# A two-level Strassen product at the end of a fused attention and feed-forward kernel: five store buffers, earlier differences, a PSUM bank read out in another way

## The chip, the cores and the metric

The kernel runs on one core of a Trainium2 chip. The metric is the device time of one execution in microseconds, and the time given for a kernel is the median of several executions. A profiled execution also has a span, from its first instruction to its last; its own time is a little longer than that.

The engines are named as the profile names them: PE (TensorE, matmuls), PEld (its weight loads), DVE (VectorE), ACT (ScalarE), POOL (GpSimd) and SP (SyncE, here only an issuer of DMAs). [...]

## The reference

```
q, k, v: (8, 12, 448, 64) float32; w_in: (768, 2048); w_out: (2048, 768)
q_n, k_n = rmsnorm(q, g_q), rmsnorm(k, g_k)
attn = softmax(q_n @ k_n^T / sqrt(64)) @ v          # per batch and head
x = attn.transpose(0, 2, 1, 3).reshape(3584, 768)
h = x @ w_in
out = relu(h)^2 @ w_out                             # (3584, 768) float32
```

What matters here is the last line: g = relu(h)^2 times w_out.

## The kernel before, in words

The eight batches are taken two at a time, in four spans of 896 tokens. For each span the kernel computes attention, then the first product (x times w_in, with the activation, giving g), then the second product (g times w_out). Both products use the Winograd form of Strassen's algorithm with seven products of half-size blocks instead of eight: g is cut into g11, g12, g21 and g22 by feature halves and batches. It lies transposed in `gT` (16 rows of features, each with 448 tokens of the one batch and 448 of the other), and the differences of g that the form needs lie in `gC` (three sets of eight rows).

In spans 0 to 2 the second product of a span is spread under the attention of the next. In span 3 no attention is left, and `last_product` computes the second product alone. It applies the Winograd form a second time, inside each of the seven products, to two of the three output column blocks of 128; the third column block is computed plainly. The change is in this function.

`last_product` runs its seven products in the order A11, A12, S2, S1, S3, A22, S4 (`order`, index `o`). For each of them PE runs, in this order:

- **pa** (a11 times b11: 8 matmuls of 224 columns), which ACT copies to p1i (L1264);
- **the third block** `ps`, 16 matmuls of 448 columns (`third`, L1235), which DVE or ACT adds or copies into its place (L1239 and L1241);
- **pb**, **pc** and **pd**, 8 matmuls each, with the sums of weights s1 to s4 and the differences of g t1 to t4;
- then **pa** again (a12 times b21 on top of the first value), **pd** again (a22 times t4 on top) and **pc** again (s4 times b22 on top).

DVE makes zi = p1i + pb (L1275) and yi = zi + pc (L1279). `based` (L1254) lets POOL add the base, a block of an earlier product's result, to these: za and zb from zi, yb from yi. `meet` (L1247) is the DVE addition that takes one quarter out of PSUM: yb + pd after pd's first use, base + pa, za + pd after its second use, zb + pc. PE may only run pd a second time when the addition yb + pd has read the bank, since the second use adds to the value in it. In the product S3 (`both`) the quarters go to two extra buffers, `blocks`, and POOL adds these to two bases (`settle`, L1259).

Around this core, for the next product: `add_g` (L1191) makes one of the four differences of g on DVE (896 elements wide, into `ts`), `add_weights` (L1179) makes the four sums of weights on POOL, and `load_set` (L1170) fetches a set of weights of w_out by a DMA on SP. `combine` makes the differences in `gC` from one row of g: four DVE instructions of 448 elements, two in part 0 (L1028 and L1029) and two in part 1 (L1031 and L1032).

`deliver` sends one finished block to HBM: DVE transposes it in squares of 32 into a store buffer `osb` (L1139), and four DMAs of 56 KB each take it out (L1142). The pool has two such buffers. The blocks m = 1 and 0 of a product that leaves are delivered "late", in the next product behind the third block's sum; the third block itself is sent at once. In the last product (`end`) the blocks go as soon as they are there, with the DMAs on SP and ACT in turn, and block 0 in two halves.

The order of instructions on each engine is the order in which the code issues them. Waits between engines and for buffers come from the tile framework.

Of the kernel before, what the change touches and what calls it, by code (L numbers as in the profile page):

```python
# [10 lines left out]
F32 = mybir.dt.float32  # L11
# [376 lines left out]
def attention_then_ffn_bounded(  # L388
# [35 lines left out]
    nc = tc.nc  # L424

    B, H, S, D = q.shape
    NT, DM = out.shape
    DFF = w_in.shape[1]
    P = 128
# [3 lines left out]
    NFC = DFF // P  # L433
    HALF = DM // 2
    HC = NPAIR // 2
    HF = NFC // 2
    NSPAN = B // 2
# [27 lines left out]
    qk, qkT, ident, mhalf, gains, rstd0, _ = held  # L465
    gT = consts.tile([P, NFC, 2 * S], F32, name="gT")
    xT = consts.tile([P, 2, NPAIR, S], F32, name="xT")
    xC = consts.tile([P, 3, HC, S], F32, name="xC")
    gC = consts.tile([P, 3, HF, S], F32, name="gC")
# [24 lines left out]
    A11, S2, S1, S3, A12, A22, S4 = range(7)  # L494
# [526 lines left out]
    def combine(f, parts=(0, 1)):  # L1021


        g11, g12 = gT[:, f, 0:S], gT[:, f, S:2 * S]
        g21, g22 = gT[:, HF + f, 0:S], gT[:, HF + f, S:2 * S]
        sub = nc.vector.tensor_tensor
        if 0 in parts:
            sub(gC[:, 0, f], g12, g11, ALU.subtract)  # L1028
            sub(gC[:, 1, f], g22, gC[:, 0, f], ALU.subtract)  # L1029
        if 1 in parts:  # L1030
            sub(gC[:, 2, f], g21, gC[:, 1, f], ALU.subtract)  # L1031
            sub(g12, g22, g12, ALU.subtract)  # L1032
# [101 lines left out]

    rows = out.rearrange("(b g t) n -> b t g n", b=B, t=32)

    def deliver(work, span, ct, col, t, queues=(nc.sync,), part=slice(0, S // 32)):
        osb = work.tile([P, S // 32, 32], F32, tag="osb", name="osb")[:, part]
        nc.vector.transpose(osb.rearrange("p g n -> p (g n)"), ct[:, part.start * 32:part.stop * 32])  # L1139
        for i in range(0, P, 32):  # L1140
            queue = queues[i // 32 % len(queues)]
            queue.dma_start(rows[2 * span + t, :, part, col * P + i:col * P + i + 32], osb[i:i + 32])  # L1142

    def last_product(pool):
# [4 lines left out]
        HK, HS = HF // 2, S // 2  # L1149
# [5 lines left out]
        left = [[qf[:, NW2:NW2 + NS], qf[:, NW2 + NS:NW2 + 2 * NS], tf[:, 0:NS], tf[:, NS:2 * NS]],  # L1155
                [xf[:, 4 * NT2 + n * NS:4 * NT2 + (n + 1) * NS] for n in range(3)] + [tf[:, 2 * NS:3 * NS]]]
        ts = [[t[:, n * NT2:(n + 1) * NT2].rearrange("p (c n) -> p c n", c=HK) for n in range(4)] for t in (cf, xf)]
        dead = [gT[:, f, 0:S] for f in range(NFC)]
        used, late = [0], []
        sub, add = ALU.subtract, ALU.add  # L1160

        def weights_of(o, m, k):
# [18 lines left out]
        def parts_of(o):  # L1181
            rhs = rhs_of[order[o]]
            return [[rhs[:, k * HK:(k + 1) * HK, t * HS:(t + 1) * HS] for t in range(2)] for k in range(2)]

        def add_g(o, n):
            if o == len(order):
                return
            (b11, b12), (b21, b22) = parts_of(o)
            t1, t2, t3, t4 = ts[o % 2]
            dst, x, y = ((t1, b12, b11), (t2, b22, t1), (t3, b22, b12), (t4, b21, t2))[n]  # L1190
            nc.vector.tensor_tensor(dst, x, y, sub)  # L1191
# [4 lines left out]
        work = yield load_set, add_weights, add_g  # L1196

        p1s = [work.tile([P, S], F32, tag="p1", name="p1", bufs=HC) for _ in range(HC)]
        ys = dead[0:HC]
        blocks = [work.tile([P, S], F32, tag="block", name="block") for _ in range(2)]  # L1200

        def place():
            used[0] += 1
            return dead[HC - 1 + used[0]]

        def run(ps, lhs, rhs, first=True):
            for c in range(HK):
# [4 lines left out]
        for o, i in enumerate(order):  # L1212
            end = o + 1 == len(order)
            (b11, b12), (b21, b22) = parts_of(o)
            (a11, a12), (a21, a22) = [[weights_of(o, m, k) for k in range(2)] for m in range(2)]
            s1, s2, s3, s4 = sums_of(o)
            t1, t2, t3, t4 = ts[o % 2]

            into = {A11: [(None, p1s)], A12: [(p1s, None)], S2: [(p1s, p1s)], S1: [(p1s, ys)],
                    S3: [(ys, None), (p1s, p1s)], A22: [(p1s, None)], S4: [(ys, None)]}[i]  # L1220
            leaves = any(dst is None for _, dst in into)
            into = [(base, dst or [place() for _ in range(HC)]) for base, dst in into]
            at = ((HC if i in (S3, A22) else 0), 1 if i in (S3, S4) else 0)

            def send(m, part=slice(0, S // 32)):
                deliver(work, NSPAN - 1, into[0][1][m], m + at[0], at[1],
                        (nc.sync, nc.scalar) if end else (nc.sync,), part)

            both = len(into) > 1

            def third():
                m = HC - 1
                ps = bank("ps")
                for c in range(HF):
                    nc.tensor.matmul(ps, weights_of(o, m, c // HK)[:, c % HK], rhs_of[i][:, c],  # L1235
                                     start=c == 0, stop=c == HF - 1)
                for base, dst in into:
                    if base is None:
                        nc.scalar.copy(dst[m], ps)  # L1239
                    else:  # L1240
                        nc.vector.tensor_tensor(dst[m], base[m], ps, add)  # L1241

            def meet(m, t, left, ps):

                part = slice(t * HS, (t + 1) * HS)
                dst = blocks[m] if both else into[0][1][m]
                nc.vector.tensor_tensor(dst[:, part], left, ps, add)  # L1247

            def based(m, t, x, name):
                base = into[0][0]  # L1250
                if both or base is None:
                    return x
                y = small_of(name)
                nc.gpsimd.tensor_tensor(y, x, base[m][:, t * HS:(t + 1) * HS], add)  # L1254
                return y

            def settle(m):
                for base, dst in into if both else ():
                    nc.gpsimd.tensor_tensor(dst[m], base[m], blocks[m], add)  # L1259

            pa = ps_s.tile([P, 2, 512], F32, tag="s", name="pa")[:, 0, 0:HS]
            run(pa, a11, b11)
            p1 = small_of("p1i")
            nc.scalar.copy(p1, pa)  # L1264
            third()
            add_g(o + 1, 0)
            for args in late:
                deliver(*args)
            late[:] = []
            if leaves:  # L1270
                send(HC - 1)
            pb = ps_o.tile([P, S], F32, tag="o", name="pb")[:, 0:HS]
            run(pb, s2, t2)
            z, y = small_of("zi"), small_of("yi")
            nc.vector.tensor_tensor(z, p1, pb, add)  # L1275
            z21, z12 = based(1, 0, z, "za"), based(0, 1, z, "zb")
            pc = bank("pc")[:, 0:HS]
            run(pc, s1, t1)
            nc.vector.tensor_tensor(y, z, pc, add)  # L1279
            y22 = based(1, 1, y, "yb")  # L1280
            add_g(o + 1, 1)
            pd = ps_o.tile([P, S], F32, tag="t", name="pd")[:, 0:HS]
            run(pd, s3, t3)
            add_weights(o + 1)
            meet(1, 1, y22, pd)
            run(pa, a12, b21, False)
            if both or into[0][0] is None:
                nc.scalar.copy((blocks if both else into[0][1])[0][:, 0:HS], pa)
            else:
                meet(0, 0, into[0][0][0][:, 0:HS], pa)  # L1290
            add_g(o + 1, 2)
            run(pd, a22, t4, False)
            meet(1, 0, z21, pd)
            settle(1)
            if end:
                send(1)
                send(0, slice(0, HS // 32))
            run(pc, s4, b22, False)
            meet(0, 1, z12, pc)
            settle(0)  # L1300
            if end:
                send(0, slice(HS // 32, S // 32))
            elif leaves:
                for m in (1, 0):
                    late.append((work, NSPAN - 1, into[0][1][m], m + at[0], at[1]))
            add_g(o + 1, 3)
            load_set(o + 2)
        yield

# [66 lines left out]
    with tc.tile_pool(name="last_product", bufs=2, reuse_waits="tile") as last:  # L1376
        rest = last_product(last)
        load_set, add_weights, add_g = next(rest)
        with tc.tile_pool(name="first_product", bufs=2, reuse_waits="tile") as work:
            for u, _ in enumerate(first_product(work, NSPAN - 1)):  # L1380
                if u in (14, 21):
                    load_set(u // 7 - 2)
                if u == N1 // 2:
                    add_weights(0)
                if u == N1 - 2:
                    add_g(0, 0)
                    add_g(0, 1)
                if u == N1 - 1:
                    add_g(0, 2)
                    add_g(0, 3)  # L1390
                    combine(HF - 1)
        with tc.tile_pool(name="second_product", bufs=2, reuse_waits="tile") as work:
            rest.send(work)

# [87 lines left out]
```

## Time and profile before

| | us |
|---|---|
| median of 3 runs | 1368.57 (1367.56 to 1369.83) |
| the profiled execution's own time | 1369.07 |
| its span | 1367.1 |
| PE busy | 1335.5 (98%) |
| DVE, ACT, POOL busy | 875.6, 431.8, 627.2 |
| mean granted PE clock | 0.992 |
| first matmul of the last product | 1227.68 |
| last matmul's modelled end | 1357.81 |

The profile gives every instruction with its start, its duration and, in brackets, how long its engine stood idle before it and what ended that. The ends of matmuls are modelled. A table of stretches gives each engine's busy time between two moments, with the clock that was granted to PE (1.00 is full speed).

### The profile page before, as it was taken

Reading aid. Unit: us, or ns where it says so; the run is one execution under the profiler, and the core shown is the slowest. Engines: PE = TensorE matmul, PEld = TensorE weight load, DVE = VectorE, ACT = ScalarE, POOL = GpSimd, SP = SyncE. Lnnn points to the kernel's source line nnn. Section 1 sums busy time; section 2 is a strip of 40 time slices with the busy share of each in tenths; the row PEclk is TensorE's granted clock in tenths of the full one; section 3 lists DMA queues with packets and bytes.
Section 4 is the critical chain, followed back from the end, with each engine's and each line's share of the span. In section 5 each row is a group of like instructions: output and inputs, shape, how many; then the busy total and the mean of one; then the engine's idle time right before and its main releaser. Section 6 shows DMA issues by size and latency. Waiting matters only on the chain.

```text
span 1367.1 us, 17241 instructions
## 1 busy us (share of the span) xinstructions
PE 1335.5 (98%) x5770; PEld 671.9 (49%) x5770; DVE 875.6 (64%) x1535; ACT 431.8 (32%) x681; POOL 627.2 (46%) x505
## 2 busy tenths in 40 slices
PE   8999999999999999999999999999999999999986
PEld 3333445444444554544444455444444455557865
DVE  6999788599987334477788423467787623336442
ACT  7886466433332111233333011233333111110000
POOL 5667533466573123555564122645666312424541
PEclk9999999999999999999999999999999999999997
DMA  9777999655675333355676433344765435312332
GB/s 239 214 220 197 319 362 322 181 128 109 132 149 128 97 88 90 100 114 123 141 143 119 111 93 90 100 109 108 153 125 115 102 99 182 87 58 67 111 101 37
DMA packets 413815, 190.15 MB, mean 139 GB/s; under 512 B 282389, under 2 KB 408725, under 8 KB 413717
## 3 DMA queue, kind: packets, MB, share of 16 engines
q1 hardware_dynamic: 406164, 180.21, 51.0%
q0 software_dynamic: 4736, 8.40, 2.5%
q8 instruction: 48, 0.79, 0.2%
q10 hardware_dynamic: 2816, 0.34, 0.2%
q14 instruction: 51, 0.41, 0.1%
HBM read 155.72 MB, written 33.16 MB: 138 GB/s over the span
## 4 chain that ended last, share of the span: by engine, by line
PE 87%; DVE 7%; ACT 2%; issue 1%; DMA 1%; POOL 1%; SPq 0%; DVEq 0%; ACTq 0%; POOLq 0%
PE ps L1106 28%; PE pd L1068 10%; PE pa L1068 10%; PE pc L1068 10%; PE sc L785 7%; PE pav L862 7%; PE pb L1068 5%; PE ps L1235 3%; PE pd L1208 1%; ACT gT L797 1%; PE pc L1208 1%; PE pa L1208 1%; DVE gT L810 1%; PE sc L793 1%; DVE rstd L715 1%
## 5 line engine op out<-in xcount | busy, mean ns | idle before, releaser
L1106 PE MATMUL ps<-gT,sw 128*128 128x448 f32 x576 | 225.8, 543 | 0.0
L1044 POOL TENSOR_TENSOR gT<-gT 128x448 f32<-128x448 f32 x96 | 93.7, 978 | 284.6 <-ACT gT L1040 284.6
L750 POOL TENSOR_TENSOR half<-half,mhalf 128x28 f32<-128x28 f32 x36 | 176.1, 4891 | 71.7 <-DVE half L749 68.5
L1106 PE MATMUL ps<-gC,sw 128*128 128x448 f32 x432 | 170.1, 543 | 0.0
L1106 PEld LDWEIGHTS ps<-gT,sw 128*128 128x128 f32 x576 | 107.5, 190 | 113.9 <-issue 110.2
L1068 PE MATMUL pa<-xT,sw 128*128 128x448 f32 x384 | 155.0, 540 | 0.6 <-ACT p L1072 0.6
L1040 ACT ACTIVATE gT<-gT 128x448 f32<-128x448 f32 x96 | 55.3, 577 | 313.9 <-DVE gT L1083 313.9
L1106 PEld LDWEIGHTS ps<-gC,sw 128*128 128x128 f32 x432 | 80.6, 190 | 86.3 <-issue 83.7
L787 ACT ACTIVATE pr<-sc 128x896 f32<-128x896 f32 x87 | 77.5, 915 | 121.8 <-PE sc L785 121.8
L785 PE MATMUL sc<-qkT 64*64 64x448 f32 (+1 forms) x1152 | 109.7, 496 | 0.0
L1068 PEld LDWEIGHTS pa<-xT,sw 128*128 128x128 f32 x384 | 72.8, 190 | 72.7 <-issue 70.5
L583 POOL TENSOR_TENSOR gC<-gC 128x384 f32<-128x384 f32 x64 | 76.4, 1212 | 62.1 <-DVE gC L579 60.4
L1083 DVE TENSOR_TENSOR gT<-z,pd 128x448 f32<-128x448 f32 x32 | 19.8, 620 | 97.8 <-PE pd L1068 97.7
L830 POOL DMA_DIRECT2D xT<-factors x72 | 38.1, 534 | 92.3 <-DMA factors<-square 55.3
L1068 PE MATMUL pd<-xT,sw 128*128 128x448 f32 x192 | 77.9, 542 | 1.4 <-DVE z L1075 1.4
L1068 PE MATMUL pd<-xC,sw 128*128 128x448 f32 x192 | 77.5, 540 | 1.3 <-DVE gT L1083 1.3
L1068 PE MATMUL pb<-xC,sw 128*128 128x448 f32 x192 | 77.5, 540 | 0.2 <-DVE gT L1083 0.2
L1068 PE MATMUL pc<-xC,sw 128*128 128x448 f32 x192 | 77.4, 539 | 0.0
L1068 PE MATMUL pc<-xT,sw 128*128 128x448 f32 x192 | 77.4, 539 | 0.0
L752 POOL TENSOR_TENSOR qk<-qk,half 128x448 f32<-128x448 f32 x72 | 75.5, 1068 | 2.8
L862 PE MATMUL rest<-pr,vt 64*64 64x448 f32 x348 | 72.7, 537 | 0.0
L862 PE MATMUL pav<-pr,vt 64*64 64x448 f32 x348 | 72.7, 537 | 0.0
(223 smaller groups left out, 2176.8 us busy)
## 6 DMA issues: line engine op xcount, KB each, us to landing
sw<-w1s SPq DMA_DIRECT2D x224, 192.0 KB, 2.4
sw<-w2s SPq DMA_DIRECT2D x126, 256.0 KB, 3.3
w1s<-gC SPq DMA_DIRECT2D x8, 1344.0 KB, 7.2
w2s<-gC SPq DMA_DIRECT2D x8, 1344.0 KB, 6.2
out_dram<-osb SPq DMA_DIRECT2D x184, 56.0 KB, 1.8
qk<-in_q_dram SPq DMA_DIRECT2D x144, 56.0 KB, 3.6
qk<-in_k_dram SPq DMA_DIRECT2D x144, 56.0 KB, 2.9
xT<-factors POOLq DMA_DIRECT2D x72, 112.0 KB, 3.4
```

Source lines behind the costliest of these rows:

```text
L583: nc.gpsimd.tensor_tensor(*[blocks_of(n)[:, place_of(n, i)] for i in (dst, x, y)], op)
L750: nc.gpsimd.tensor_tensor(half, half, mhalf, ALU.pow)
L752: nc.gpsimd.tensor_tensor(qkn[:, s], raw[:, s], half[:, s * NG:(s + 1) * NG].rearrange("p g -> p g ()").to_broadcast([P, NG, 32]), ALU.mult)
L785: nc.tensor.matmul(sc[part, h, 0:n], qkT[rows, 0, 1, keys], qkT[rows, 0, 0, of], start=True, stop=True)
L787: nc.scalar.activation(pr, sc[:, :, 0:n], AF.Exp)
L862: nc.tensor.matmul(into, vs[i][rows, h, c, :], probs[i, c][rows, h, :], start=(c == 0), stop=(c == NF), skip_group_check=True)
L1040: nc.scalar.activation(g, src, AF.Relu)
L1044: nc.gpsimd.tensor_tensor(g, g, g, ALU.mult)
L1068: nc.tensor.matmul(ps, stream[n + at][:, c], rhs[:, c], start=first and c == 0, stop=c == HC - 1, skip_group_check=not first)
L1106: nc.tensor.matmul(ps, stream[n][:, c % 4], rhs_of[i][:, c], start=c == 0, stop=c == HF - 1)
L1208: nc.tensor.matmul(ps, lhs[:, c], rhs[:, c], start=first and c == 0, stop=c == HK - 1, skip_group_check=not first)
L1235: nc.tensor.matmul(ps, weights_of(o, m, c // HK)[:, c % HK], rhs_of[i][:, c], start=c == 0, stop=c == HF - 1)
```

## The change

The change does five things in `last_product` and `deliver`:

1. The store buffer `osb` of the last product gets five buffers instead of two (`kept`).
2. Three differences of g for the next product are issued ahead of the third block, and so are the late deliveries; the fourth comes behind yi.
3. Where a product has a base and one destination, pd is read out by adding the base to it; y is added to the result afterwards, in place, on POOL (on DVE in the last product). yb is gone.
4. The results of A12, S3, A22 and S4 and the two `blocks` get fixed rows of `gT` and `gC` that are no longer read; the separate `block` buffers are gone.
5. The second part of `combine` for the last row of g moves from ahead of the last product to the end of its first stage.

```diff
-    def deliver(work, span, ct, col, t, queues=(nc.sync,), part=slice(0, S // 32)):
-        osb = work.tile([P, S // 32, 32], F32, tag="osb", name="osb")[:, part]
+    def deliver(work, span, ct, col, t, queues=(nc.sync,), part=slice(0, S // 32), kept=2):
+        osb = work.tile([P, S // 32, 32], F32, tag="osb", name="osb", bufs=kept)[:, part]
...
-        dead = [gT[:, f, 0:S] for f in range(NFC)]
-        used, late = [0], []
+        dead = [gT[:, f, 0:S] for f in range(HF)] + [gC[:, 1, f] for f in range(HF)]
+        late = []
...
-        blocks = [work.tile([P, S], F32, tag="block", name="block") for _ in range(2)]
-
-        def place():
-            used[0] += 1
-            return dead[HC - 1 + used[0]]
+        blocks = dead[2 * HF - 2:]
+        homes = {A12: dead[HC:2 * HC], S3: dead[HF:HF + HC], A22: dead[HF + HC:HF + 2 * HC], S4: dead[HC:2 * HC]}
...
-            into = [(base, dst or [place() for _ in range(HC)]) for base, dst in into]
+            into = [(base, dst or homes[i]) for base, dst in into]
...
             run(pa, a11, b11)
             p1 = small_of("p1i")
             nc.scalar.copy(p1, pa)
-            third()
-            add_g(o + 1, 0)
+            for n in range(3):
+                add_g(o + 1, n)
             for args in late:
                 deliver(*args)
             late[:] = []
+            third()
             if leaves:
                 send(HC - 1)
...
             nc.vector.tensor_tensor(y, z, pc, add)
-            y22 = based(1, 1, y, "yb")
-            add_g(o + 1, 1)
+            add_g(o + 1, 3)
             pd = ps_o.tile([P, S], F32, tag="t", name="pd")[:, 0:HS]
             run(pd, s3, t3)
             add_weights(o + 1)
-            meet(1, 1, y22, pd)
+            if both or into[0][0] is None:
+                meet(1, 1, y, pd)
+            else:
+                meet(1, 1, into[0][0][1][:, HS:S], pd)
+                x = into[0][1][1][:, HS:S]
+                (nc.vector if end else nc.gpsimd).tensor_tensor(x, x, y, add)
             run(pa, a12, b21, False)
...
-            add_g(o + 1, 2)
             run(pd, a22, t4, False)
...
-                    late.append((work, NSPAN - 1, into[0][1][m], m + at[0], at[1]))
-            add_g(o + 1, 3)
+                    late.append((work, NSPAN - 1, into[0][1][m], m + at[0], at[1], (nc.sync,), slice(0, S // 32), 5))
+            if o == 0:
+                combine(HF - 1, (1,))
             load_set(o + 2)
...
-                    combine(HF - 1)
+                    combine(HF - 1, (0,))
```

`send` passes the five buffers to `deliver` in the same way.

More of the change, by code (lines that the diff above doesn't have):

```diff
@@ L1226, in send @@
                 deliver(work, NSPAN - 1, into[0][1][m], m + at[0], at[1],
-                        (nc.sync, nc.scalar) if end else (nc.sync,), part)
+                        (nc.sync, nc.scalar) if end else (nc.sync,), part, 5)
             both = len(into) > 1
```

## The prediction

> **What bounds the kernel now.** I looked first at the page: TensorE (PE) is busy for 1335.5 of 1367.1 us, so whatever PE does not wait for is free. The change touches only the last product and what leads into it, so I cut that end of the trace at the starts of its seven pa blocks (numbered stage 0 to 6 below) and asked for busy times by stretch. Columns: stretch, length, then busy time of PE, weight loads, VectorE (DVE), ScalarE (ACT), GpSimd (POOL), granted clock, DMA share and GB/s.
>
> ```profile
> span 1367.1 us, 17241 instructions
> ...
> 1227.68:1246.26 18.58, 16.88 (x74) 13.55 (x73) 16.50 (x16) 1.69 (x4) 8.38 (x6) 1.00 0.03 4
> 1246.26:1262.93 16.67, 16.67 (x73) 13.55 (x72) 7.88 (x12) 0.35 (x1) 6.27 (x6) 1.00 0.37 110
> 1262.93:1280.06 17.13, 16.87 (x73) 13.55 (x73) 8.80 (x13) 0.35 (x1) 9.27 (x8) 1.00 0.43 118
> 1280.06:1296.67 16.61, 16.61 (x73) 13.64 (x73) 8.17 (x11) 0.35 (x1) 9.64 (x8) 1.00 0.29 97
> 1296.67:1313.28 16.61, 16.61 (x74) 13.64 (x74) 7.67 (x12) 0.69 (x2) 9.49 (x7) 1.00 0.36 109
> 1313.28:1336.81 23.53, 19.14 (x74) 15.39 (x73) 9.92 (x14) 0.35 (x1) 12.80 (x11) 0.85 0.35 94
> 1336.81:1357.81 21.00, 18.72 (x73) 14.72 (x71) 6.41 (x13) 0.35 (x1) 1.89 (x3) 0.92 0.23 36
> 1357.81:1367.10 9.29, 0.00 (x0) 0.00 (x0) 0.80 (x2) 0.00 (x0) 0.00 (x0) 0.61 0.36 55
> ```
>
> Stages 3 and 4 never wait: 16.61 us, which is seven blocks of 1.51 and the third block's 6.01. The others show what can be won: 1.97 in stage 0, 0.06 in stage 1, 0.52 in stage 2, 6.92 in stage 5, 4.22 in stage 6 (against 16.78, since its last block is counted to its modelled end), and the 9.29 after PE's last matmul. The timeline of PE says where each loss sits: always at the second use of the pd bank.
>
> ```profile
> 1243.12 1.78 PE L1208 MATMUL pd<-xC,qk 128*128 128x224 f32 x8 [1.70 <-DVE p L1247]
> 1276.93 1.78 PE L1208 MATMUL pd<-xC,qk 128*128 128x224 f32 x8 [0.26 <-DVE p L1247]
> 1331.41 3.36 PE L1208 MATMUL pd<-xT,wb 128*128 128x224 f32 x8 [4.39 <-DVE gT L1247]
> 1352.83 3.12 PE L1208 MATMUL pd<-xC,qk 128*128 128x224 f32 x8 [2.28 <-DVE gT L1247]
> ```
>
> All wait for L1247, the addition that reads pd's first value (`meet(1, 1)`); PE may not add to the bank before it. VectorE's own timeline says what held that addition back in the last two stages, and what held the last store back:
>
> ```profile
> 1327.14 0.65 DVE L1139 STREAM_TRANSPOSE osb<-gT 128x448 f32<-128x448 f32 x1 [3.43 <-DMA out_dram<-osb]
> ...
> 1330.97 0.39 DVE L1247 TENSOR_TENSOR gT<-yb,pd 128x224 f32<-128x224 f32 x1 [1.16 <-POOL yb L1254]
> ...
> 1352.38 0.39 DVE L1247 TENSOR_TENSOR gT<-yb,pd 128x224 f32<-128x224 f32 x1 [1.51 <-POOL yb L1254]
> ...
> 1361.16 0.41 DVE L1139 STREAM_TRANSPOSE osb<-gT 128x224 f32<-128x224 f32 x1 [2.93 <-DMA out_dram<-osb]
> ```
>
> The third delivery of a stage waits until one of two store buffers has left (3.43 us); zi, yi, then GpSimd's za, zb, yb queue up behind it. That is one chain: buffer, zi, yb, pd.
>
> **What the Trainium skill says.** "SBUF — State Buffer", "Who interferes with whom": a VectorE instruction with two SBUF inputs contends with a GpSimd instruction that reads SBUF; the loser blocks for the whole of the other's instruction. The trace agrees, and this sets my price for stage 0:
>
> ```profile
> 1236.80 1.57 DVE L1031 TENSOR_TENSOR gC<-gT,gC 128x448 f32<-128x448 f32 x1
> 1238.29 1.68 DVE L1032 TENSOR_TENSOR gT<-gT 128x448 f32<-128x448 f32 x1
> ...
> 1236.24 1.65 POOL L1179 TENSOR_TENSOR xT<-wb 128x512 f32<-128x512 f32 x1
> 1237.85 1.65 POOL L1179 TENSOR_TENSOR qkT<-wb,xT 128x512 f32<-128x512 f32 x1
> ```
>
> The same two instructions take 0.62 us at 1226.2. Beside GpSimd, each ends 0.48 after the GpSimd instruction does, and GpSimd's next ends some 1.15 later: they alternate. "TensorE: Matmul & The Clock Gate", "What's actually happening": a free-running window of about 3.4 us; one that is idle halves PE's clock until a busy one has passed. Here too, with a threshold:
>
> ```profile
> 1325.80:1329.20 3.40, 1.22 (x7) 0.87 (x5) 1.96 (x4) 0.00 (x0) 1.00 (x2) 1.00 0.65 100
> 1329.20:1332.60 3.40, 1.19 (x3) 1.12 (x4) 2.24 (x4) 0.00 (x0) 3.32 (x4) 0.50 0.34 55
> 1240.40:1243.80 3.40, 1.70 (x10) 1.35 (x9) 3.30 (x6) 0.35 (x1) 0.00 (x0) 1.00 0.00 0
> ```
>
> A window with 1.22 us of work (2.2 idle) was followed by half clock; one with 1.70 (1.7 idle) was not.
>
> **The change, part by part.**
>
> *Five store buffers.* Stages 5 and 6 deliver three and six blocks; the wait was for a transfer of two deliveries ago (landing 1.9 us after issue, four issues of 0.49 on SP). With five, only the sixth delivery of stage 6 reuses one, of some 15 us before. The waits of 3.43, 3.23 and 2.93 go. Late next in stages 5 and 6: nothing, see pd.
>
> *pd freed without GpSimd.* VectorE adds the base to pd at once (0.39, one SBUF input, so no lock). GpSimd's yb (0.66) becomes an in-place addition of y (0.66), queued behind `add_weights` (four of 1.3 to 2.0); in stage 6 VectorE does it, 0.39, beside PE's pa. With B as the end of pb: zi ends at B+0.4, yi at B+1.9, the base goes on at the end of pd, B+3.0, done by B+3.4; PE wants pd at B+4.5. So stages 2, 5 and 6 lose nothing: **−0.52, −6.92, −4.22**, half clock of stages 5 and 6 included. Who waits for the late addition: only the next stage's transposes of that block, after stages 1 and 5. GpSimd ends it near B+8.7; VectorE comes to the transposes at B+8 (stage 6) to B+11; the third sum behind them is due at B+15.1. Covered by the third block's 6.01; without it, up to 0.7.
>
> *Differences ahead.* Three 896-wide instructions (1.08 each alone, up to twice that beside GpSimd) and two transposes (0.6) fill 4.5 to 6.5 of the 7.5 us until the third sum is ready, where VectorE stood idle for 5.4 to 6.2. Free there. The eight DMAs of a late delivery keep their place on SP: behind the last `load_set`, ahead of the third block's four; they pass nothing. The fourth difference (index 3) takes the place of the second between yi and `meet(1, 1)`. There `add_weights` starts as zb ends (B+1.75), so the difference waits for one GpSimd instruction (to B+3.0), ends at B+4.0, and the base addition ends at B+4.4 against 4.5. On a knife's edge: 0 to 0.3 in each of stages 1, 2, 3, 5; I take **+0.3** in all.
>
> *Stage 0 gets worse.* Behind the combine's first half (ends 1236.76) stood two 448-wide subtractions and one difference before zi; now three differences. In the alternating pattern: first behind GpSimd's third weight sum (1237.89 + 0.97), GpSimd's fourth (1240.04), second (1241.0), third (1242.0); it was 1240.98. So zi, yi, the fourth difference and pd come 1.0 later: **+1.0** (bounds 0 and +1.5). PE's idle time becomes 2.7, and half clock may follow. In this execution's window 1240.4 to 1243.8 only 1.0 of work would be left, under the 1.22 above. Over free phases, with a threshold of 2.0 idle, (3.41 + 2.7 − 4.0) / 3.41 = 62%. It halves some 3 us of work: **+1.5** when it comes. The combine's second half (two of 0.62) at the end of stage 0 takes the place of a 1.08 difference; stage 1 has 7 us free: 0.
>
> *Results in rows of g, blocks too.* The rows now used (gC's second third after S2; gT's first rows after A11) were last read a stage or more earlier, so no wait: 0 (bounds 0 and +0.5). No instruction is added.
>
> *The tail.* It is 9.29: 0.4 for the sum, 2.93 waiting for a buffer, 0.41 transpose, 0.9 for two issues on each of SP and ACT, 2.5 landing, 2.6 to the end. The wait goes, but the last four DMAs then stand behind the eight just before: on each queue 0.3, 1.46 (this trace's odd long one; 0.49 normally), 0.5, 0.5 from E−0.4, E being the modelled end of the last matmul; so they issue at E+1.4 to 2.4 and the end comes at E+6.8 to 7.8. "DMA: Bandwidth & Descriptors", "Issuing engines are not separate DMA queues", says that SP and ACT share the 16 engines; that costs little here: the eight DMAs before the last four made up some 2.5 us of full DMA share (0.13, 0.72, 0.51, 0.99 and 0.10, microsecond by microsecond from 1357). Taken: 7.3, **−2.0** (−1.5 to −2.5).
>
> Sum: 1.0 + 1.5 + 0.3 − 0.52 − 6.92 − 4.22 − 2.0 = −10.9. The profiled execution took 1369.07 (span and 1.97 around it), so 1358.2; it stands 0.5 above the median of the three runs, 1368.57. In their terms **1357.7 us**.
>
> **Rivals.**
> - *No half clock in stage 0*: 1.5 less, 1356.2. The window's phase decides; 1.0 of work against 1.22 speaks for the half clock.
> - *Stage 0 hardly grows*, if VectorE gets two turns to GpSimd's one: 1355. Against it: the strict alternation above.
> - *The knife's edge cuts*: a second GpSimd instruction (1.3) slips in before the fourth difference in stages 1, 2, 3 and 5, each costing about 1: 1361.5. The alternation speaks against it.
> - *It doesn't do what it says*: the third delivery still waits some 3.4 us in stage 5, for SP's queue of issues instead of a buffer: 1361. SP has 5.8 us of issues there (12 of 0.49), but VectorE needn't wait for issues, only for free buffers.
> - *Slower*: GpSimd's late addition stands behind `add_weights`, and that behind the next set's transfer. If it comes after B+15, VectorE stops at the late transposes with the third sum, zi and pd behind it, in stages 2 and 6. From 6.4 us of delay on it costs one for one; to turn the 12 us won into a loss it must be 13 late in each. The only such wait shown is 2.45 (a set landing 6.5 after issue). At 13 late: about 1371.
>
> **How the numbers follow.** The forecast has 0.48, no half clock 0.27, stage 0 unchanged 0.08, knife's edge 0.10, stores still waiting 0.04, slower 0.03. Likeliest case alone: 1356.7 to 1359. Adding the others until under 2 in 10 is left out: 1354.5 to 1361. What a measurement can tell from no change is about 0.2%, 2.7 us; every case but the last is beyond it, with a little left for two bad ones together: faster 0.95, same 0.02, slower 0.03.
>
> **What would show it.** Right: no transpose waiting for out_dram; stages 2 to 6 at 16.6 to 16.8; stage 0 at 19.5, or 21 at half clock; GpSimd gone from pd's waits; under 8 us after the last matmul. Wrong: a wait at pd over 0.5 in a stage other than 0, a stage 0 under 18.6, or VectorE waiting for GpSimd at a late transpose.

## The result, and the profile after

The changed kernel takes 1360.93 us (median of 5, 1359.77 to 1361.38) against 1368.57 (median of 5): a ratio of 0.994, with a 95% interval of 0.9926 to 0.9955. It is faster by 0.6%, clear of noise, and inside the range of the prediction (1354.5 to 1361), but by less than 0.1 us: it lies 3.2 us above the forecast of 1357.7.

The profiled execution took 1361.38, with a span of 1359.1. Cut at the starts of the seven pa blocks as before (same columns: stretch, length, busy time of PE, weight loads, DVE, ACT, POOL, granted clock, DMA share, GB/s):

```profile
1228.54:1249.49 20.95, 18.27 (x74) 14.69 (x72) 16.49 (x15) 1.69 (x4) 8.89 (x6) 0.92 0.03 4
1249.49:1266.20 16.71, 16.71 (x74) 13.56 (x74) 9.75 (x14) 0.34 (x1) 6.86 (x6) 1.00 0.36 110
1266.20:1282.93 16.73, 16.73 (x73) 13.55 (x72) 9.14 (x13) 0.34 (x1) 7.58 (x8) 1.00 0.44 122
1282.93:1299.64 16.71, 16.71 (x74) 13.56 (x74) 8.01 (x11) 0.34 (x1) 7.60 (x8) 1.00 0.27 95
1299.64:1316.24 16.60, 16.60 (x73) 13.63 (x72) 7.64 (x12) 0.69 (x2) 6.60 (x7) 1.00 0.35 109
1316.24:1332.85 16.61, 16.61 (x73) 13.64 (x73) 11.26 (x14) 0.35 (x1) 11.94 (x10) 1.00 0.51 132
1332.85:1349.62 16.77, 16.77 (x73) 13.45 (x72) 6.10 (x13) 0.35 (x1) 2.35 (x4) 1.00 0.28 44
1349.62:1359.10 9.48, 0.00 (x0) 0.00 (x0) 0.80 (x2) 0.00 (x0) 0.00 (x0) 0.71 0.35 55
```

Stages 5 and 6, which took 23.53 and 21.0, are at the floor (16.61, and 16.78 for stage 6). Stage 0 has grown from 18.58 to 20.95. The tail, forecast at 7.3, is 9.48: it has not shrunk at all. PE waits for pd in stage 0 alone.

Stage 0 in the timeline. The first three lines are the three differences that now stand ahead of zi, then the two sums of weights on GpSimd that run beside them, then PE's second use of pd:

```profile
1237.57 2.18 DVE L1191 TENSOR_TENSOR xT<-gT 128x896 f32<-128x896 f32 x1
...
1239.78 2.04 DVE L1191 TENSOR_TENSOR xT<-gT,xT 128x896 f32<-128x896 f32 x1
...
1241.75 1.08 DVE L1191 TENSOR_TENSOR xT<-gT 128x896 f32<-128x896 f32 x1
...
1237.12 1.68 POOL L1179 TENSOR_TENSOR xT<-wb 128x512 f32<-128x512 f32 x1
...
1238.76 2.12 POOL L1179 TENSOR_TENSOR qkT<-wb,xT 128x512 f32<-128x512 f32 x1
...
1244.97 3.17 PE L1205 MATMUL pd<-xC,qk 128*128 128x224 f32 x8 [2.68 <-DVE p L1244]
```

Two differences take 2.18 and 2.04 us beside GpSimd, and the third takes 1.08 once GpSimd is done: the engines take turns. PE stands for 2.68 us and then runs its eight matmuls in 3.17 instead of 1.78, for the most part at half clock.

The tail in the view of who waited for whom on SP's queue, from 1340 us on (total, times, longest):

```profile
SPq L1142 <- DVE osb L1139: 10.2, 3, 6.8
SPq L1142 <- DMA out_dram<-osb: 1.5, 2, 1.1
```

No transpose waits for a transfer any more; instead the issue of one DMA waits for the landing of another. The trace names for each DMA its semaphore, the counter that its landing raises: the twelve of the tail share eight. SP's issue at 1352.93 takes over the semaphore of a DMA that ACT issued at 1349.32, and starts 0.02 us after that one has landed, at 1352.91. It is not the number under way that holds it. SP begins to wait at 1351.78, when six are under way and two of the eight semaphores are free; those two go to ACT's next issues, at 1351.84 and 1352.40. The one buffer wait became two semaphore waits, 1.5 us together.

### The profile page after: what moved, and what is told of

Its sections match the earlier page's. It is cut to its first block, busy times and chain, and to the rows that moved or that the text cites. A ratio compares the mean times of both kernels' runs of the same rounds, so it can differ in the third digit from the quotient of the medians.

```text
span 1359.1 us, 17239 instructions
## 1 busy us (share of the span) xinstructions
PE 1334.0 (98%) x5770; PEld 671.3 (49%) x5770; DVE 875.7 (64%) x1536; ACT 431.7 (32%) x681; POOL 621.4 (46%) x504
## 4 chain that ended last, share of the span: by engine, by line
PE 89%; DVE 6%; ACT 3%; issue 1%; DMA 0%; POOL 0%; DVEq 0%; ACTq 0%
PE ps L1106 28%; PE pd L1068 10%; PE pa L1068 10%; PE pc L1068 10%; PE sc L785 7%; PE pav L862 7%; PE pb L1068 5%; PE ps L1232 3%; PE pd L1205 2%; PE pc L1205 1%; PE pa L1205 1%; ACT gT L797 1%; DVE gT L810 1%; PE sc L793 1%; DVE rstd L715 1%
```

## The experiments

Each kernel was timed in five rounds beside the kernel before, and ratios are to that. Stages are those of its profiled execution.

**Is it the order in stage 0?** (e1) The changed kernel with:

```diff
-            for n in range(3):
+            for n in range(3) if o else ():
                 add_g(o + 1, n)
...
-            add_g(o + 1, 3)
+            if o:
+                add_g(o + 1, 3)
...
             if o == 0:
+                for n in range(4):
+                    add_g(1, n)
+            if o == 1:
                 combine(HF - 1, (1,))
```

> The changed kernel, but in stage 0 no difference of g stands ahead of the third block: all four for the next product come at the end of stage 0, and the combine's second half for the last row comes at the end of stage 1 instead of stage 0. Theory (stage 0 pays for differences that VectorE makes in turn with GpSimd's sums of weights, and then for half clock): stage 0 falls from 20.95 us to 16.6 to 17.0, no half clock follows, stage 1 stays within 0.3 of 16.71; in all 4.0 to 4.4 us less than the changed kernel, some 1356.7. Rival (pd's first value is late in stage 0 for another reason, such as the g rows that the last squares on GpSimd leave late): stage 0 stays above 19, in all less than 2 us gained.

Measured: 1355.57 us, ratio 0.9901 (0.9885 to 0.9916). Stage 0 by stretch, and VectorE in it:

```profile
1226.87:1243.48 16.61, 16.61 (x74) 13.63 (x73) 10.50 (x11) 1.69 (x4) 8.04 (x6) 1.00 0.03 5
```

```profile
1234.37 1.58 DVE L1029 TENSOR_TENSOR gC<-gT,gC 128x448 f32<-128x448 f32 x1
1236.18 0.39 DVE L1273 TENSOR_TENSOR zi<-p1i,pb 128x224 f32<-128x224 f32 x1 [0.22 <-PE pb L1205]
1237.62 0.39 DVE L1277 TENSOR_TENSOR yi<-zi,pc 128x224 f32<-128x224 f32 x1 [1.06 <-PE pc L1205]
```

VectorE now waits for PE, not the other way round, and stage 0 is at its floor: 4.34 us less than in the changed kernel, and 1.97 less than before. Both the old loss and the new one were differences and combines in VectorE's way. The four differences fit behind it: stage 1 takes 16.70. The median fell by 5.4 us, 1.0 more than I expected at most; the stages and the tail account for 4.4 of it, and the last product began 1.7 us earlier in this profile, which is within the scatter of its start (see the end of the next section).

**What holds the tail: DMAs under way, or bytes?** (e2) The changed kernel with block 0 of the last product sent whole, after the last matmul: the same bytes, later, in eight DMAs instead of twelve.

```diff
             if end:
                 send(1)
-                send(0, slice(0, HS // 32))
...
             if end:
-                send(0, slice(HS // 32, S // 32))
+                send(0)
```

> The changed kernel, but block 0 of the last product leaves whole after the last matmul, in four DMAs, instead of in two halves with four DMAs each: eight DMAs in the tail instead of twelve, with the same bytes, and the first half leaving later. Theory A (the tail stayed at 9.5 us because the ninth and later DMAs wait until an earlier one, whose semaphore they take over, has landed: eight can be under way): no DMA waits for another, the tail falls from 9.48 to 7.2 to 8.0 us, in all 1.5 to 2.3 less. Theory B (bytes: the 16 DMA engines with pieces of 128 bytes are the bound): the tail is the same or longer, 9.5 to 10.5, since the bytes start later.

Measured: 1358.84 us, 0.9922 (0.9908 to 0.9935). The tail by stretch:

```profile
1350.05:1357.77 7.72, 0.00 (x1) 0.00 (x0) 1.03 (x2) 0.00 (x0) 0.00 (x0) 0.77 0.45 68
```

9.48 has become 7.72, though the first half of block 0 starts later. The bytes are not the bound. SP waits for no landing in it, as theory A said, but four issues are gone too, and e2 does not part the two. The record of the queues gives an estimate: the last issue ends 5.12 us after the last matmul in the changed kernel and 3.09 here, and SP's two waits are 1.5 of these 2.03.

(e3) The other way: each half as soon as it is there, in sixteen DMAs.

```diff
                 (nc.vector if end else nc.gpsimd).tensor_tensor(x, x, y, add)
+            if end:
+                send(1, slice(HS // 32, S // 32))
...
                 meet(0, 0, into[0][0][0][:, 0:HS], pa)
+            if end:
+                send(0, slice(0, HS // 32))
...
-                send(1)
-                send(0, slice(0, HS // 32))
+                send(1, slice(0, HS // 32))
```

> The changed kernel, but in the last product each half of blocks 1 and 0 leaves as soon as it is there (four deliveries of four small DMAs each, in the order 1 right, 0 left, 1 left, 0 right). Theory A (eight DMAs under way at most): the first two groups have landed when the third and fourth want their semaphores, so the tail falls from 9.48 to 6.0 to 7.0 us, in all 2.5 to 3.5 less. Theory B (bytes): the bytes start about 2 us earlier, so the tail falls too, to 7 to 8.5. A third possibility (the issue cost of 0.5 us for each DMA decides): 16 instead of 12 issues, the tail stays at 9 or more.

Measured: 1361.05 us, 0.9932 (0.9918 to 0.9945); the tail is 9.97. My own numbers for theory A missed: I had the first groups landed in time. They were not, since both queues draw on the same semaphores, and SP's first DMA of the tail, at 1349.62, had to wait for one that ACT had issued 3.0 us before. SP's queue from 1340 us on:

```profile
SPq L1142 <- DMA out_dram<-osb: 10.5, 3, 4.9
```

Of the three possibilities the third gave the right tail, but not for its reason alone. Of the 10.5 us of waiting for landings only 0.8 falls behind the last matmul; the other waits held SP back before it. So SP's eight issues, which take 4.4 us together, nearly all came behind the last matmul, and the last of them ended 5.5 us after it. With 8, 12 and 16 DMAs the tails are 7.7, 9.5 and 10.0; but the number does not decide alone: the runs with twelve go from 9.29 (before) to 11.35 (e5). In every run the end comes 4.1 to 5.0 us after the last issue has ended.

**Which part brought the gain?** (e4) The changed kernel with two buffers and with yb on GpSimd again. What is left is the order, and the places of results.

```diff
-                        (nc.sync, nc.scalar) if end else (nc.sync,), part, 5)
+                        (nc.sync, nc.scalar) if end else (nc.sync,), part, 2)
...
             nc.vector.tensor_tensor(y, z, pc, add)
+            y22 = based(1, 1, y, "yb")
             add_g(o + 1, 3)
...
-            if both or into[0][0] is None:
-                meet(1, 1, y, pd)
-            else:
-                meet(1, 1, into[0][0][1][:, HS:S], pd)
-                x = into[0][1][1][:, HS:S]
-                (nc.vector if end else nc.gpsimd).tensor_tensor(x, x, y, add)
+            meet(1, 1, y22, pd)
...
-                    late.append((work, NSPAN - 1, into[0][1][m], m + at[0], at[1], (nc.sync,), slice(0, S // 32), 5))
+                    late.append((work, NSPAN - 1, into[0][1][m], m + at[0], at[1], (nc.sync,), slice(0, S // 32), 2))
```

> The changed kernel with two of its parts undone: two store buffers again, and yb again on GpSimd ahead of pd; only the new order (three differences and the late deliveries ahead of the third block) and the new places of results are left. Theory A (the order alone lets the late deliveries leave early, so the buffer wait comes while PE works, and zi is early enough that GpSimd's yb is covered): stages 1 to 4 and 6 at 16.6 to 17.0, stage 5 at most 1.5 us longer, tail within 0.7 of 9.48; in all 0 to 2.5 us slower than the changed kernel. Theory B (the prediction's parts: the buffers bring the 3.43 and 3.23 of waiting, pd without GpSimd the rest): stages 5 and 6 go back to some 20 us or more, in all 6 to 11 us slower.

Measured: 1361.02 us, 0.9946 (0.9932 to 0.996), not to be told from the changed kernel's 0.994. Stages 3, 5 and 6:

```profile
1280.21:1296.82 16.61, 16.61 (x74) 13.64 (x73) 7.53 (x11) 0.35 (x1) 7.71 (x8) 1.00 0.27 97
...
1313.43:1331.16 17.73, 16.87 (x74) 13.55 (x73) 11.30 (x14) 0.34 (x1) 11.51 (x10) 1.00 0.47 123
1331.16:1347.91 16.75, 16.75 (x73) 13.43 (x71) 5.61 (x12) 0.34 (x1) 3.33 (x5) 1.00 0.28 44
```

The order alone does nearly all: 5.80 of the 6.92 in stage 5, everything in stage 6. My parts list had given these to the buffers and to pd. (The new places of results and the moved half of `combine` are in this run too; no run has the order without them.)

(e7) The changed kernel with two buffers, pd read out in the new way.

```diff
-                        (nc.sync, nc.scalar) if end else (nc.sync,), part, 5)
+                        (nc.sync, nc.scalar) if end else (nc.sync,), part, 2)
...
-                    late.append((work, NSPAN - 1, into[0][1][m], m + at[0], at[1], (nc.sync,), slice(0, S // 32), 5))
+                    late.append((work, NSPAN - 1, into[0][1][m], m + at[0], at[1], (nc.sync,), slice(0, S // 32), 2))
```

> The changed kernel with two store buffers again and pd read out in the new way. Theory (with the late deliveries ahead of the third block, the third delivery's wait for a buffer falls on time that the new pd path has in hand, and the tail is set by DMAs under way): stage 5 at 16.6 to 16.9, where the order alone had 17.73, stage 6 at 16.8, tail 9.0 to 10; in all within 1 us of the changed kernel. Rival (the five buffers are needed): stage 5 over 18 or the tail over 10.5, in all over 1.5 us slower than the changed kernel.

Measured: 1360.28 us, 0.9944 (0.993 to 0.9957). Stage 5 is 16.61, stage 6 is 16.77, the tail 10.02. VectorE still waits for a buffer in stage 5, and PE does not notice:

```profile
1324.97 0.65 DVE L1139 STREAM_TRANSPOSE osb<-gC 128x448 f32<-128x448 f32 x1 [2.00 <-DMA out_dram<-osb]
```

So against e4 the new pd path is worth 1.1 us in stage 5. It gives 0.3 back in stages 1 to 3, which take 16.71, 16.74 and 16.71 here and 16.61 each in e4. The five buffers, where the order is new, bring nothing that can be seen: 0.9944 and 0.994. With two, the buffer wait is back in the tail (3.87 us), and SP waits for no landing there. PE's gap in stage 0 is the same as in the changed kernel, but this time no half clock follows:

```profile
1244.72 1.78 PE L1205 MATMUL pd<-xC,qk 128*128 128x224 f32 x8 [2.67 <-DVE p L1244]
```

Its stage 0 takes 19.54, against 20.95 after a gap of 2.68: half clock costs 1.4 us. The profiled executions of the changed kernel, e2, e3 and e4 have it, e7 does not. What differs is where the gap falls. The changes of the granted clock lie whole windows of 3.413 us apart: in the changed kernel it changes at 1244.41, 1247.82 and 1353.63, which is 1 and then 31 windows. In e7 it changes at 1353.27, and 32 windows before that is 1244.04. Here are the window that ends there and the next one, first in the changed kernel and then in e7:

```profile
1241.00:1244.41 3.41, 1.29 (x7) 0.94 (x5) 3.31 (x5) 0.35 (x1) 0.00 (x0) 1.00 0.00 0
1244.41:1247.82 3.41, 2.85 (x8) 2.60 (x9) 0.50 (x2) 0.00 (x0) 0.00 (x0) 0.50 0.00 0
...
1240.63:1244.04 3.41, 1.42 (x8) 1.07 (x6) 3.31 (x5) 0.35 (x1) 0.00 (x0) 1.00 0.00 0
1244.04:1247.46 3.42, 2.74 (x14) 2.74 (x15) 1.02 (x3) 0.00 (x0) 0.00 (x0) 1.00 0.00 0
```

A window with 1.29 us of PE work was followed by half clock, one with 1.42 was not; the prediction's threshold (2.0 idle, so 1.41 of work) lies between. How the windows lie to the gap changes from execution to execution, and so does the price of the gap.

(e5) The kernel before with more store buffers alone.

```diff
-    def deliver(work, span, ct, col, t, queues=(nc.sync,), part=slice(0, S // 32)):
-        osb = work.tile([P, S // 32, 32], F32, tag="osb", name="osb")[:, part]
+    def deliver(work, span, ct, col, t, queues=(nc.sync,), part=slice(0, S // 32), kept=2):
+        osb = work.tile([P, S // 32, 32], F32, tag="osb", name="osb", bufs=kept)[:, part]
...
-                        (nc.sync, nc.scalar) if end else (nc.sync,), part)
+                        (nc.sync, nc.scalar) if end else (nc.sync,), part, 4)
...
-                    late.append((work, NSPAN - 1, into[0][1][m], m + at[0], at[1]))
+                    late.append((work, NSPAN - 1, into[0][1][m], m + at[0], at[1], (nc.sync,), slice(0, S // 32), 4))
```

> The kernel before with four store buffers instead of two in the last product and nothing else changed (five don't fit beside its other buffers; with four, no delivery takes a buffer over that left less than 10 us ago). Theory (one serial chain of buffer, third delivery, zi, yb, pd: cutting it at its head frees the rest): no transpose waits for a transfer; stage 5 falls from 23.53 to 16.6 to 18.2 us (yb may still be up to 1.5 late), stage 6 from 21.0 to 16.8 to 17.2, stage 0 stays at 18.6, the tail stays at 9 to 10 because of the DMAs under way; in all 8.5 to 11 us less than before, some 1359. Rival (GpSimd's yb is a bound of its own): stage 5 stays above 20 and stage 6 above 18.5, in all less than 6 us less.

Measured: 1361.64 us, 0.9949 (0.9935 to 0.9962). Stages 5 and 6 fall as the chain theory said:

```profile
1313.11:1330.83 17.72, 16.88 (x74) 13.56 (x74) 9.81 (x14) 0.34 (x1) 10.66 (x10) 1.00 0.46 123
1330.83:1347.60 16.77, 16.77 (x73) 13.45 (x71) 6.66 (x13) 0.34 (x1) 4.88 (x5) 1.00 0.29 44
```

What is left in stage 5 is yb:

```profile
1327.25 0.39 DVE L1247 TENSOR_TENSOR gT<-yb,pd 128x224 f32<-128x224 f32 x1 [1.16 <-POOL yb L1254]
```

The tail is 11.35, longer than before's 9.29, which I had not expected; SP's queue there:

```profile
SPq L1142 <- DMA out_dram<-osb: 6.2, 2, 5.4
```

The longest wait is that of a store of the third block. It stands on SP from 1345.25 to 1350.65, 3.05 us past the last matmul, until the DMA that ACT issued at 1347.22 has landed, whose semaphore it takes over. The tail's own six issues on SP stand behind it, and the last of them ends 6.81 us after the last matmul, against 4.67 before: that is the 2.1 that the tail is longer. The stages gave 9.6 us, with 0.4 lost in stage 4 that I did not pursue, and 2.1 went back in the tail, which leaves 7.5 in the profiled executions. The medians are 6.7 apart, less than the 8.5 that I had as the lower bound.

(e6) The kernel before with the new way to read out pd alone.

```diff
-            y22 = based(1, 1, y, "yb")
...
-            meet(1, 1, y22, pd)
+            if both or into[0][0] is None:
+                meet(1, 1, y, pd)
+            else:
+                meet(1, 1, into[0][0][1][:, HS:S], pd)
+                x = into[0][1][1][:, HS:S]
+                (nc.vector if end else nc.gpsimd).tensor_tensor(x, x, y, add)
```

> The kernel before with pd read out by adding the base to it and y added later (on GpSimd, in the last product on VectorE), with the old order and two store buffers. Theory (the chain's head is the buffer, GpSimd is its smaller part): the transposes wait as before; stage 2 falls to 16.6; stage 5 from 23.53 to 20 to 22, since zi is still late; stage 6 from 21.0 to 17.0 to 18.5, since 0.9 us of waiting is left there and half clock may not follow; in all 4 to 7 us less than before. Rival (pd's wait for GpSimd is the main thing): stages 5 and 6 fall under 17.5, in all 10 us or more less.

Measured: 1363.28 us, 0.9965 (0.9952 to 0.9977). Stage 2 is at 16.61, stage 5 at 21.32, stage 6 at 17.99. The transposes wait as they did, and PE behind them, for less:

```profile
1324.36 0.65 DVE L1139 STREAM_TRANSPOSE osb<-gT 128x448 f32<-128x448 f32 x1 [3.06 <-DMA out_dram<-osb]
...
1345.14 0.65 DVE L1139 STREAM_TRANSPOSE osb<-gT 128x448 f32<-128x448 f32 x1 [3.51 <-DMA out_dram<-osb]
```

```profile
1327.38 3.12 PE L1208 MATMUL pd<-xT,wb 128*128 128x224 f32 x8 [2.76 <-DVE gT L1247]
...
1346.90 1.78 PE L1208 MATMUL pd<-xC,qk 128*128 128x224 f32 x8 [0.96 <-DVE gT L1247]
```

In stage 5 GpSimd was the lesser part of the chain: PE's gap falls from 4.39 to 2.76 us. In stage 6 it was the greater part, and the shorter gap there (0.96 instead of 2.28) also spares the half clock.

**A version that beats both.** (e8) e1 and e2 together, and the fourth difference issued behind the addition that reads pd instead of ahead of it.

```diff
             nc.vector.tensor_tensor(y, z, pc, add)
-            add_g(o + 1, 3)
...
                 (nc.vector if end else nc.gpsimd).tensor_tensor(x, x, y, add)
+            if o:
+                add_g(o + 1, 3)
             run(pa, a12, b21, False)
```

> The changed kernel with three alterations together: in stage 0 no difference ahead of the third block (all four at its end, the combine's second half at the end of stage 1), block 0 of the last product sent whole, and the fourth difference issued behind the addition that reads pd instead of ahead of it. Theory: stage 0 at 16.6, stages 1 to 3 at 16.6 instead of 16.7 since GpSimd's sums of weights no longer delay pd by way of the fourth difference, tail at 7.5 to 8; in all 7 us less than the changed kernel, some 1353.5. Rival (the fourth difference then delays VectorE's next reads of pa and pd): stages 1 to 3 at 16.8 or more, the rest as said.

Measured: 1353.11 us, 0.9886 (0.987 to 0.9902). Stages 0, 1, 2 and the tail:

```profile
1227.64:1244.25 16.61, 16.61 (x74) 13.64 (x72) 10.52 (x11) 1.69 (x4) 8.05 (x6) 1.00 0.03 5
1244.25:1260.86 16.61, 16.61 (x74) 13.65 (x74) 12.56 (x16) 0.34 (x1) 6.75 (x6) 1.00 0.37 110
1260.86:1277.47 16.61, 16.61 (x74) 13.64 (x73) 10.26 (x15) 0.34 (x1) 7.69 (x8) 1.00 0.43 121
...
1344.05:1351.97 7.92, 0.00 (x1) 0.00 (x0) 1.03 (x2) 0.00 (x0) 0.00 (x0) 0.83 0.43 66
```

PE waits in none of the seven stages, and the tail with eight DMAs is as short as in e2. From the first matmul of the last product to the end it is 124.33 us, against 130.56 in the changed kernel and 139.42 before.

## Why the prediction was right, and where it was off

- **The number**: inside the range by luck. The measured 1360.93 misses the 1356.7 to 1359 that the prediction gave for its likeliest case alone. The range went up to 1361 for other cases (stores still waiting at 1361, and a second GpSimd instruction ahead of the fourth difference at 1361.5), and none of these occurred; what used up the room was the tail.
- **Which stages gain**: right. Stages 2, 5 and 6 were to come down by 0.52, 6.92 and 4.22; they came down by 0.40, 6.92 and 4.23.
- **Why they gain**: right as a chain, wrong in its shares. The prediction credited the buffers with the head of the chain and pd's new path with its end, and priced the new order at nothing won. e4 shows the order alone to bring nearly all, and e5 the buffers alone nearly as much in the stages. In the medians the buffers alone bring 6.7 us, pd's path alone 5.1 and the order alone 8.1, and all together 7.6: a cut at the head of a serial chain frees what follows, so the parts' gains do not add up.
- **Stage 0**: right. Forecast +1.0 for the queue and +1.5 for half clock; the idle time of PE went from 1.70 to 2.68 (forecast 2.7), and the stage grew by 2.37. The Trainium skill's rule in "SBUF — State Buffer", "Who interferes with whom", carried this step, and the two differences beside GpSimd (2.18 and 2.04 instead of 1.08) agree with it. The 62% for the half clock was an estimate from the window length in "TensorE: Matmul & The Clock Gate", "What's actually happening", and a threshold from the trace; four of the five profiled executions with this gap had the half clock, and e7 shows why one had not.
- **Knife's edge**: right. +0.3 for stages 1, 2, 3 and 5 together; above the floor of 16.61 they measured 0.10, 0.12, 0.10 and 0.00, in all 0.32. e8, with the fourth difference moved, shows it gone.
- **The tail**: this is the step that failed. The term "−2.0 (−1.5 to −2.5)" measured +0.2. The prediction saw that the last four DMAs would stand behind the eight ahead of them and priced their issue, but put at nothing that an issue must wait for the landing of the DMA whose semaphore it takes over. It had the last issues at 1.4 to 2.4 us after the last matmul; SP's last two came 4.1 and 4.4 after it, with 1.5 us of such waiting on that queue. From the last issue to the end it was 5.1 us, as before. In the profile of before SP waits for no landing: its last four DMAs come at 1361.60 and later, behind the buffer wait, and by then the earlier DMAs on their semaphores have landed (1359.92 and 1360.09, where the trace tells it). (The pieces that the prediction names for before's 9.29 add up to 9.74, since landing is counted from the start of an issue. That is not what failed.)
- **Its own signs**: two of those named came out against it. The tail is over 8 us, and VectorE waits for GpSimd at a late transpose in stage 6, for 0.45 us. The second cost nothing, since VectorE stands for the third block's product for 5.45 us right after:

```profile
1333.96 1.17 DVE L1139 STREAM_TRANSPOSE osb<-gC 128x448 f32<-128x448 f32 x2 [0.45 <-POOL gC L1287]
1340.58 0.62 DVE L1238 TENSOR_TENSOR gT<-gT,ps 128x448 f32<-128x448 f32 x1 [5.45 <-PE ps L1232]
```

- **The rest of the 3.2 us**, between profiled executions (1361.38 against 1358.2): 2.2 is the tail, 0.86 lies ahead of the last product, whose first matmul came at 1228.54 instead of 1227.68, and 0.3 outside the span; the stages gave 0.2 more than forecast. The first matmul's time scatters from 1225.7 to 1227.7 over the three profiles with the order of before, and from 1225.8 to 1228.8 over the seven others, where the code ahead of it is the same, so the 0.86 cannot be put down to the change.

## What to carry to other kernels

When a matmul waits at the end of a serial chain, look for the earliest cheap cut: moving independent work into the engine's own idle time did here what more buffers and a shorter path did too, and doing all three paid only once. When work is moved ahead, check the one stage in which the engine has no idle time: the same order that freed stages 5 and 6 cost stage 0 2.4 us. And look at the issues of DMAs at the end of a kernel: when a buffer wait is removed, the next wait may be for the semaphore of a DMA that another queue issued, and fewer, larger DMAs can end sooner.

## What the runs showed that I had not expected

- The stores of the tail share eight semaphores over both queues, and an issue stands until the DMA that had its semaphore before has landed, also when that one came from the other queue and while other semaphores are free. This cost SP 1.5 us in the changed kernel's tail, and one wait of 5.4 us in e5.
- A DMA issue of 0.3 to 0.5 us took 1.2 to 1.7 us once on each queue in most of the profiles, when SP and ACT issued stores at the same time (1.46 before, 1.53 after, 1.29 in e2, on SP). In e1 and e5 only ACT's queue had such a long one, and in e6 neither: its longest took 0.68. No run tells its cause, and it stays open.
- The same gap of PE, 2.68 and 2.67 us, was followed by half clock in one execution and not in another: 20.95 against 19.54 us for one stage. The window of 3.41 us in which it fell had 1.29 us of work in the one and 1.42 in the other.
